# Attention and two MLPs on one core: fewer DMAs, a shorter warm-up, and VectorE casting the high part of v

## The chip, the cores and the metric

The kernel runs on one core of one Trainium2 chip. The metric is the device time of one execution in microseconds. Five engines work side by side, each through its own instructions in order: TensorE (matrix products, into PSUM), VectorE, ScalarE and GpSimd (element by element), and SyncE (SP), which here only issues DMAs.

## The reference

```
scores = q @ k^T / sqrt(64)                    # 2 x 12 heads, 448 x 448
scores = cap * tanh(scores / cap)
attn = softmax(scores) @ v                     # -> x, 896 tokens x 768
x = elu(x @ w_in1) @ w_out1                    # 768 -> 2048 -> 768
out = relu(x @ w_in2) ** 2 @ w_out2            # 768 -> 2048 -> 768
```

The weights are 64-bit floats; q, k, v are 32-bit.

## The kernel before

Every product is made of three: a value is split into a high part (cast to a shorter format, float32r) and a low part (value minus high part), and high x high, high x low and low x high are added in PSUM. ScalarE and VectorE make the parts.

The attention takes two heads at a time, a *pair*; there are 12, and two pairs share a *group* of loads. Round n of the loop at L572 holds, for pair n, tanh and exp on ScalarE (`tanh`, `exp`: e), the split of the probabilities on VectorE (`split_p`: cast ph, subtraction pl, in two parts) and the products with v on TensorE (`pv`, into po); for pair n + 1, the low part of k and q (`low`: kql), the two parts of v (`prep_v`: vh, vl) and the first scores (`scores`: sc); for pair n + 2, the transposition of k and q (`turn`, into the one PSUM tile pt, which `high` on ScalarE and `low` on VectorE read). The last block of v has 64 rows and goes its own way (`vs`, kz and qz are the like of k and q).

The softmax's denominators fall out of `pv` as an extra row. `pv_out(n - 1)` copies po to pvs on ScalarE and a DMA brings the row to 64 partitions (den). A round later `norm(n - 2)` takes the reciprocal on VectorE (rd), writes it to DRAM by a DMA (far) and reads it back to all partitions by two DMAs (bc). A round later still `norm_x(n - 3)` multiplies (xn) and splits x into xh and xl.

The order is written out by hand (`manual_schedule`): the text of the loop is the order on each engine. All DMAs but the very first are on SP's queue, in this order in a round: far and the two bc of `norm`, in rounds 2 to 6 one weight load (`ws.load`), den of `pv_out`, then the loads of `load_group`: k and q (with kz, qz) and the tail of v in even rounds, v in odd ones.

Weights come in chunks (`Stream`): a load, then six steps on VectorE and ScalarE that turn 64-bit floats into a high and a low part (and or absolute value, clamp, shift, sign, low, high, rest). Two chunks are worked whole on VectorE during the attention (`ws.whole`, the second in round 1, between `low` and the split of the probabilities), the others step by step (`ws.advance`). `prep_v` is on GpSimd: for n > 1 a copy of one column (gate) that waits for VectorE's pl, the cast vh and the subtraction vl. At the start `idle_products` are matrix products that nobody reads.

After round 11 the tail (L621 to L651) finishes pairs 9, 10 and 11 (`norm`, `norm_x`) among the first products of the first MLP (`mm_in`), which need x of all pairs at their end. From there on the MLPs run on TensorE with the weight chunks made beside them.

Of the kernel before, what the change touches and what calls it, by code (L numbers as in the profile page):

```python
# [26 lines left out]
def attention_moe_kernel(  # L27
# [63 lines left out]
    gate = one.tile([P, 1], F32, name="gate")  # L91
# [12 lines left out]
    def load_group(g, what="kqvw", pp=None, dma=nc.sync.dma_start):  # L104
# [6 lines left out]
        if g not in nat:  # L111
            nat[g] = {x: lp.tile([P, NFULL, 4, D], F32, name=x, tag=x) for x in "kq"}
            nat[g]["v"] = lp.tile([P, 4, NFULL, D], F32, name="v", tag="v")
# [19 lines left out]
        if "v" in what:  # L133
            for hh in range(h0, h0 + nh):
                dma(
                    nat[g]["v"][:, hh],
                    v[b, 2 * hp + hh, :NFULL * P].rearrange("(c p) d -> p c d", p=P),
                )
# [7 lines left out]
    def prep_v(n):  # L146
        if n >= len(pairs):
            return
        g, pp = divmod(n, 2)
        vh, vl = vhs[n % 3], vls[n % 3]  # L150
        if n > 1:


            nc.gpsimd.tensor_copy(gate, st["p", n - 2][1][:, NB - 2, S - 1:].bitcast(F32))
        vn = nat[g]["v"][:, 2 * pp:2 * pp + 2]
        h, l = (t.rearrange("p (c h) d -> p h c d", h=2)[:, :, :, :D] for t in (vh, vl))
        nc.gpsimd.tensor_copy(h, vn)
        nc.gpsimd.tensor_tensor(l, vn, h.bitcast(F32), op=ALU.subtract)
# [22 lines left out]

    def high(n):
        if n >= len(pairs):
            return
        st["qk", n] = [ap_.tile([P, 2, W], F32R, name=x, tag=x) for x in ("kqh", "kql")]
        nc.scalar.copy(st["qk", n][0], st["pt", n])

    def low(n):
        if n >= len(pairs):
            return  # L190
        h, l = st["qk", n]
        nc.vector.tensor_tensor(l, st["pt", n], h.bitcast(F32), op=ALU.subtract)
# [109 lines left out]
    def norm(n):  # L302


        if n < 0:
            return
        den = st["den", n]
        rd = ap_.tile([D, 2 * S // D], F32, name="rd", tag="rd")
        nc.vector.reciprocal(rd, den)
        far = dp.tile([D, 2 * S // D], F32, name="far", tag="far")  # L310
        nc.sync.dma_start(far, rd)
        bc = ap_.tile([D, 2, S], F32, name="bc", tag="bc")
        flat = far.rearrange("p s -> (p s)")
        for u in range(2):
            src = flat[u * S:(u + 1) * S].unsqueeze(0).to_broadcast([D, S])
            nc.sync.dma_start(bc[:, u], src)
        st["bc", n] = bc
# [25 lines left out]
    class Stream:  # L343
# [119 lines left out]
        def whole(self):  # L463

            self.alone = True
            self.open(self.done)
            emit(self.begin(self.done) + self.end(self.done))
            self.done += 1
            self.alone = False
            self.hold = 0  # L470
# [62 lines left out]
    with tc.manual_schedule():  # L533
# [24 lines left out]
        ws.whole()  # L558
# [13 lines left out]
        for n in range(np_):  # L572
# [11 lines left out]
            if n == 1:  # L584
                ws.whole()
# [3 lines left out]
            if n:  # L589
                turn(n + 2)  # L590
            else:
                idle_products(ps1.tile([P, 2, W], F32, name="po", tag="po"), 20)
            norm(n - 2)
            if 2 <= n < 7:
                ws.load()
# [3 lines left out]
            pv_out(n - 1)  # L599
            tanh(n, 3)  # L600
            exp(n, 1)
            emit(norm_x(n - 3))
            split_p(n, 0)
            scores(n + 1, 0)
# [9 lines left out]
            if n % 2:  # L614
                load_group((n + 3) // 2, "v")
            else:
                load_group(n // 2 + 2, "kq")
# [4 lines left out]
        late_kc = 2 * (KC - 1)  # L622
        emit(ws.advance())
# [4 lines left out]
        norm(np_ - 2)  # L628
# [3 lines left out]
        mm_in(0, 0, begun[0], xh, xl, kb[1:7:2])  # L632
        norm(np_ - 1)
        ws.settle()
        mm_in(0, 1, begun[1], xh, xl, kb[0::2])
        emit(norm_x(np_ - 2))
# [170 lines left out]
```

## Time and profile before

| | |
|---|---|
| time, median of 3 runs | 599.96 us (599.31 to 600.51) |
| the profiled execution | 600.64 us, its span 598.9 us |
| TensorE busy | 585.6 us (98% of the span) |
| VectorE busy | 425.2 us (71%) |
| ScalarE busy | 334.9 us (56%) |
| GpSimd busy | 38.9 us (6%) |
| SP's and ScalarE's DMAs | 64.76 MB, mean 108 GB/s |

The span runs from the first to the last instruction. Busy times are shares of the whole span; the attention (up to about 142 us) and the MLPs behind it have different loads. In the rows, PE is TensorE, DVE VectorE, ACT ScalarE, POOL GpSimd, SPq the queue of SP; a row of the timeline gives start, duration, engine, line, operation, destination and sources, shapes, and in brackets how long the engine had stood idle and what ended that.

### The profile page before, as it was taken

The page shows a single profiled execution, that of the slowest core. Times are in us where ns is not written, and L with a number is a line of the kernel's source. Part 1 is how long each engine was busy: PE and PEld are TensorE (multiplying, and loading weights), DVE is VectorE, ACT ScalarE, POOL GpSimd, SP SyncE. Part 2 cuts the span into 40 slices and gives each one's busy share as a digit, 9 for nine tenths or more (in the row PEclk, how much of TensorE's full clock was granted, in tenths as well). Part 3 has the DMA queues.
Part 4 walks back from the last instruction along what each step waited for, and adds up shares of the span by engine and source line. Part 5 has one row for each costly group of instructions (what it writes and reads, how often), then busy time and mean ns, then how long its engine had stood idle before and what let it go on. Part 6 is the DMA issues. An engine that isn't in the chain of part 4 may idle for free.

```text
span 598.9 us, 8667 instructions
## 1 busy us (share of the span) xinstructions
PE 585.6 (98%) x3084; PEld 530.2 (89%) x3084; DVE 425.2 (71%) x835; ACT 334.9 (56%) x484; POOL 38.9 (6%) x66
## 2 busy tenths in 40 slices
PE   8998989989999999999999999999999999999997
PEld 8876767678999999999999999999999999999997
DVE  4777799979999888675666567777767689991000
ACT  4899789934888777543333335666666645441000
POOL 3221212100000000000000000000000011230000
PEclk9999999999999999999999999999999999999999
DMA  5644642014444333243333434333344346622000
GB/s 132 157 117 115 154 115 73 22 60 132 124 134 137 120 108 89 66 129 116 111 101 111 125 105 133 105 106 109 111 125 118 106 112 187 185 84 105 24 24 34
DMA packets 82988, 64.76 MB, mean 108 GB/s; under 512 B 38656, under 2 KB 78848, under 8 KB 82944
## 3 DMA queue, kind: packets, MB, share of 16 engines
q1 hardware_dynamic: 81440, 63.58, 37.2%
q10 hardware_dynamic: 1504, 0.62, 0.4%
q8 instruction: 24, 0.39, 0.3%
q14 instruction: 20, 0.16, 0.1%
HBM read 61.34 MB, written 2.80 MB: 107 GB/s over the span
## 4 chain that ended last, share of the span: by engine, by line
PE 84%; DVE 5%; DMA 4%; SPq 3%; ACT 2%; issue 1%; ACTq 0%; DVEq 0%
PE acc L520 19%; PE acc L521 19%; PE acc L519 19%; PE acc L738 7%; PE acc L739 7%; PE acc L737 7%; PE po L287 5%; PE sc L235 3%; DMA den<-pvs 2%; DVE pl L264 1%; SPq L120 1%; DVE xn L329 1%; ACT e L244 1%; DVE ph L263 1%; PE pt L172 1%
## 5 line engine op out<-in xcount | busy, mean ns | idle before, releaser
L521 PE MATMUL acc<-xh,wl 128*128 128x448 f32 x384 | 139.6, 364 | 2.0 <-DVE wl L443 2.0
L520 PE MATMUL acc<-xl,wh 128*128 128x448 f32 x384 | 140.0, 364 | 0.2 <-DVE xl L336 0.2
L519 PE MATMUL acc<-xh,wh 128*128 128x448 f32 x384 | 139.7, 364 | 0.2 <-ACT xh L335 0.2
L448 ACT CAST wh<-wf 128x384 fp32r<-128x384 f32 (+2 forms) x114 | 57.9, 508 | 107.6 <-PE acc L520 83.7
L393 ACT ACTIVATE wf<-wst 128x384 f32<-128x384 f32 (+2 forms) x130 | 70.4, 542 | 62.5 <-DVE wl L443 35.7
L443 DVE TENSOR_TENSOR wl<-wf,wh 128x384 fp32r<-128x384 f32 (+2 forms) x116 | 63.9, 551 | 55.3 <-ACT wh L448 55.2
L521 PEld LDWEIGHTS acc<-xh,wl 128*128 128x128 f32 x384 | 72.1, 188 | 7.6 <-DVE wl L443 2.4
L519 PEld LDWEIGHTS acc<-xh,wh 128*128 128x128 f32 x384 | 72.1, 188 | 6.2 <-ACT xh L335 0.6
L520 PEld LDWEIGHTS acc<-xl,wh 128*128 128x128 f32 x384 | 72.1, 188 | 5.7 <-DVE xl L336 0.5
L434 DVE SCALAR_TENSOR_TENSOR wf<-wst,wf 128x384 uint32<-128x384 uint32 (+3 forms) x132 | 71.9, 545 | 0.1
L427 DVE SCALAR_TENSOR_TENSOR wf<-wst,wf 128x384 uint32<-128x384 uint32 (+3 forms) x132 | 71.5, 541 | 0.1
L520 PE MATMUL acc<-gl,wh 128*128 128x448 f32 x192 | 70.0, 365 | 0.0
L521 PE MATMUL acc<-gh,wl 128*128 128x448 f32 x192 | 70.0, 364 | 0.0
L519 PE MATMUL acc<-gh,wh 128*128 128x448 f32 x192 | 69.8, 364 | 0.0
L406 DVE TENSOR_SCALAR wf<-wf 128x384 uint32<-128x384 uint32 (+3 forms) x132 | 54.5, 413 | 0.7
L402 DVE TENSOR_SCALAR wf<-wf 128x384 f32<-128x384 f32 (+3 forms) x132 | 45.9, 347 | 7.3 <-ACT wf L393 7.3
L244 ACT ACTIVATE e<-sc,tsc 128x896 f32<-128x896 f32 (+1 forms) x48 | 43.4, 910 | 6.4 <-PE sc L235 6.4
L724 DVE COPY o<-acc 128x432 f32<-128x432 f32 (+1 forms) x8 | 4.5, 558 | 53.9 <-PE acc L739 49.2
L443 POOL TENSOR_TENSOR late<-wf,late 128x336 fp32r<-128x336 f32 x16 | 15.2, 953 | 414.1 <-ACT late L448 414.1
L738 PE MATMUL acc<-wl,gh 128*128 128x432 f32 x112 | 40.3, 359 | 0.0
L739 PE MATMUL acc<-wh,gl 128*128 128x432 f32 x112 | 40.1, 358 | 0.0
L737 PE MATMUL acc<-wh,gh 128*128 128x432 f32 x112 | 40.0, 357 | 0.0
(94 smaller groups left out, 966.0 us busy)
## 6 DMA issues: line engine op xcount, KB each, us to landing
wst<-in_moe_w_in_dram SPq DMA_DIRECT2D x63, 384.0 KB, 3.2
wst<-in_moe_w_out_dram SPq DMA_DIRECT2D x24, 384.0 KB, 3.2
wst<-in_moe_w_out_dram SPq DMA_DIRECT2D x16, 432.0 KB, 3.3
wst<-in_moe_w_out_dram SPq DMA_DIRECT2D x16, 336.0 KB, 2.9
wst<-in_moe_w_out_dram SPq DMA_DIRECT2D x12, 256.0 KB, 2.7
bc<-far SPq DMA_DIRECT2D x24, 112.0 KB, 2.8
v<-in_v_dram SPq DMA_DIRECT2D x24, 96.0 KB, 2.7
k<-in_k_dram SPq DMA_DIRECT2D x15, 128.0 KB, 3.0
```

Of the source, the lines that this page charges most:

```text
L393: nc.scalar.activation(self.f[i], hi.bitcast(F32), AF.Abs)
L406: v.tensor_scalar(fb, fb, 3, 0x3FFFFFFF, op0=ALU.logical_shift_left, op1=ALU.bitwise_and)
L427: v.scalar_tensor_tensor(out=fb, in0=hi, scalar=0xC0000000, in1=fb, op0=ALU.bitwise_and, op1=ALU.bitwise_or,)
L434: v.scalar_tensor_tensor(out=fb, in0=lo, scalar=29, in1=fb, op0=ALU.logical_shift_right, op1=ALU.bitwise_or,)
L443: (v if dst is None else nc.gpsimd).tensor_tensor(wl, self.f[i], wh.bitcast(F32), op=ALU.subtract)
L448: (v.tensor_copy if self.alone else nc.scalar.copy)(wh, self.f[i])
L519: nc.tensor.matmul(acc, w[0], x[0], start=first, stop=False)
L520: nc.tensor.matmul(acc, w[0], x[1], start=False, stop=False)
L521: nc.tensor.matmul(acc, w[1], x[0], start=False, stop=last)
L737: nc.tensor.matmul(acc, gh[:, f, gs], w[0], start=a, stop=False)
L738: nc.tensor.matmul(acc, gh[:, f, gs], w[1], start=False, stop=False)
L739: nc.tensor.matmul(acc, gl[:, f, gs], w[0], start=False, stop=z)
```

## The change

- `prep_v`: for n > 1 the cast vh is made by VectorE, right behind the second part of `split_p`; the gate is gone; GpSimd makes vl.
- v is laid out by block and head instead of head and block, and a group's v comes in three DMAs (one a block) instead of four (one a head). The first group is loaded in halves and so takes six instead of four.
- From round 2 on, q of a group is loaded with v in the odd round, k alone in the even one.
- `norm` reads the reciprocals back with one DMA instead of two.
- `high` and `low` work on 960 columns instead of 1024.
- 9 idle products instead of 20 in round 0.
- The second whole weight chunk is cut in two: three instructions at the end of round 1, the other four in round 2 behind `low`.
- The weight load of rounds 2 to 6 is issued behind den instead of ahead of it.
- In the tail, `norm` of pair 10 comes first, and the product xn of pair 10 and the rest of a weight chunk come ahead of `norm` of pair 11.

```diff
-            nat[g] = {x: lp.tile([P, NFULL, 4, D], F32, name=x, tag=x) for x in "kq"}
-            nat[g]["v"] = lp.tile([P, 4, NFULL, D], F32, name="v", tag="v")
+            nat[g] = {x: lp.tile([P, NFULL, 4, D], F32, name=x, tag=x) for x in "kqv"}
...
-            for hh in range(h0, h0 + nh):
+            for c in range(NFULL):
                 dma(
-                    nat[g]["v"][:, hh],
-                    v[b, 2 * hp + hh, :NFULL * P].rearrange("(c p) d -> p c d", p=P),
+                    nat[g]["v"][:, c, h0:h0 + nh],
+                    v[b, hs, c * P:(c + 1) * P].rearrange("h p d -> p h d"),
                 )
...
-        if n > 1:
-            nc.gpsimd.tensor_copy(gate, st["p", n - 2][1][:, NB - 2, S - 1:].bitcast(F32))
-        vn = nat[g]["v"][:, 2 * pp:2 * pp + 2]
-        h, l = (t.rearrange("p (c h) d -> p h c d", h=2)[:, :, :, :D] for t in (vh, vl))
-        nc.gpsimd.tensor_copy(h, vn)
+        vn = nat[g]["v"][:, :, 2 * pp:2 * pp + 2]
+        h, l = (t.rearrange("p (c h) d -> p c h d", h=2)[:, :, :, :D] for t in (vh, vl))
+        (nc.vector if n > 1 else nc.gpsimd).tensor_copy(h, vn)
         nc.gpsimd.tensor_tensor(l, vn, h.bitcast(F32), op=ALU.subtract)
...
+    def used(t):
+        return t.rearrange("p u w -> p (u w)")[:, :W + S]
...
-        nc.scalar.copy(st["qk", n][0], st["pt", n])
+        nc.scalar.copy(used(st["qk", n][0]), used(st["pt", n]))
...
-        h, l = st["qk", n]
-        nc.vector.tensor_tensor(l, st["pt", n], h.bitcast(F32), op=ALU.subtract)
+        h, l, t = (used(x) for x in (*st["qk", n], st["pt", n]))
+        nc.vector.tensor_tensor(l, t, h.bitcast(F32), op=ALU.subtract)
...
-        flat = far.rearrange("p s -> (p s)")
-        for u in range(2):
-            src = flat[u * S:(u + 1) * S].unsqueeze(0).to_broadcast([D, S])
-            nc.sync.dma_start(bc[:, u], src)
+        flat = far.rearrange("p s -> (p s)").unsqueeze(0)
+        nc.sync.dma_start(bc.rearrange("p h s -> p (h s)"), flat.to_broadcast([D, 2 * S]))
...
-            if n == 1:
-                ws.whole()
+            if n == 2:
+                emit(second[3:])
...
-                idle_products(ps1.tile([P, 2, W], F32, name="po", tag="po"), 20)
+                idle_products(ps1.tile([P, 2, W], F32, name="po", tag="po"), 9)
             norm(n - 2)
-            if 2 <= n < 7:
-                ws.load()
...
             pv_out(n - 1)
+            if 2 <= n < 7:
+                ws.load()
...
             split_p(n, 0)
+            if n == 1:
+                second = ws.whole()
+                emit(second[:3])
...
-                load_group((n + 3) // 2, "v")
+                load_group((n + 3) // 2, "qv" if n > 1 else "v")
             else:
-                load_group(n // 2 + 2, "kq")
+                load_group(n // 2 + 2, "k" if n else "kq")
                 load_group(n // 2 + 1, "w" if n else "")
...
+        norm(np_ - 2)
         emit(ws.advance())
         ws.held = True
         split_p(np_ - 1, 1)
         mm_in(0, 0, begun[0], xh, xl, kb[6::2])
         pv(np_ - 1, 1)
-        norm(np_ - 2)
         pv_out(np_ - 1)
         emit(norm_x(np_ - 3))
         emit(ws.advance())
         mm_in(0, 0, begun[0], xh, xl, kb[1:7:2])
+        x, x_high, x_low = norm_x(np_ - 2)
+        x()
+        ws.settle()
         norm(np_ - 1)
-        ws.settle()
         mm_in(0, 1, begun[1], xh, xl, kb[0::2])
-        emit(norm_x(np_ - 2))
+        x_high()
+        x_low()
```

## Rows read from the trace of the kernel before

**Rows 1.** The page: the chain that ended last, by engine

```profile
PE 84%; DVE 5%; DMA 4%; SPq 3%; ACT 2%; issue 1%; ACTq 0%; DVEq 0%
```

**Rows 2.** Busy times by stretch: length, engines, granted clock, DMA share, GB/s

```profile
34.82:45.50 10.68, 10.68 (x68) 8.54 (x68) 8.32 (x10) 10.06 (x11) 1.67 (x3) 1.00 0.52 126
...
56.48:65.73 9.25, 8.02 (x35) 6.13 (x36) 8.14 (x11) 5.61 (x6) 1.64 (x3) 0.82 0.54 136
...
103.49:112.32 8.83, 8.72 (x49) 6.03 (x49) 8.56 (x11) 8.26 (x8) 1.65 (x3) 1.00 0.10 30
...
120.79:142.25 21.46, 18.86 (x88) 15.08 (x86) 17.37 (x34) 6.92 (x11) 0.00 (x0) 1.00 0.27 83
```

**Rows 3.** TensorE's timeline: the first scores of pairs 3 and 4

```profile
36.55 0.47 PE L235 MATMUL sc<-kqh 64*128 64x448 f32 x2
...
45.04 0.47 PE L235 MATMUL sc<-kqh 64*128 64x448 f32 x2
```

**Rows 4.** Waits from 35 to 120 us (total, times, longest), and VectorE's timeline

```profile
DVE rd L309 <- DMA den<-pvs: 8.7, 5, 2.6
...
43.13 0.23 DVE L309 RECIPROCAL rd<-den 64x14 f32<-64x14 f32 x1 [2.02 <-DMA den<-pvs]
...
54.11 0.23 DVE L309 RECIPROCAL rd<-den 64x14 f32<-64x14 f32 x1 [2.56 <-DMA den<-pvs]
```

**Rows 5.** Timeline of VectorE, rounds 8 to 10, and one row of GpSimd's

```profile
92.44 1.21 DVE L329 TENSOR_TENSOR xn<-pvs,bc 64x448 f32<-64x448 f32 x2
...
103.49 1.09 DVE L263 CAST ph<-e 128x1792 fp32r<-128x1792 f32 x1
...
108.32 1.22 DVE L192 TENSOR_TENSOR kql<-pt,kqh 128x1024 fp32r<-128x1024 f32 x1
...
109.60 1.72 DVE L329 TENSOR_TENSOR xn<-pvs,bc 64x448 f32<-64x448 f32 x2
...
109.17 1.01 POOL L158 TENSOR_TENSOR vl<-v,vh 128x384 fp32r<-128x384 f32 x1
```

**Rows 6.** Timeline of SP's queue from den of pair 1 to den of pair 2

```profile
39.29 0.50 SPq L299 DMA_DIRECT2D den<-pvs  x1
...
45.85 1.29 SPq L141 DMA_DIRECT2D vs<-in_v_dram  x2
47.23 0.56 SPq L311 DMA_DIRECT2D far<-rd  x1
48.99 1.11 SPq L316 DMA_DIRECT2D bc<-far  x2
...
50.84 0.50 SPq L299 DMA_DIRECT2D den<-pvs  x1
```

**Rows 7.** VectorE's timeline: two instructions on 384 columns, with one and two operands

```profile
26.89 0.36 DVE L448 CAST wh<-wf 128x384 fp32r<-128x384 f32 x1
...
144.45 0.55 DVE L443 TENSOR_TENSOR wl<-wf,wh 128x384 fp32r<-128x384 f32 x1
```

**Rows 8.** The start: timelines of TensorE, SP's queue and GpSimd

```profile
13.26 4.62 PE L196 MATMUL po<-ident 128*128 128x128 f32 x40
...
20.51 2.08 SPq L135 DMA_DIRECT2D v<-in_v_dram  x4
...
24.64 0.51 POOL L157 CAST vh<-v 128x384 fp32r<-128x384 f32 x1 [2.23 <-DMA v<-in_v_dram]
```

**Rows 9.** The tail: timelines of ScalarE, SP's queue, VectorE and TensorE

```profile
129.35 0.91 ACT L296 COPY pvs<-po 128x896 f32<-128x896 f32 x1 [3.20 <-PE po L287]
...
129.94 1.09 SPq L316 DMA_DIRECT2D bc<-far  x2
131.41 0.51 SPq L299 DMA_DIRECT2D den<-pvs  x1
...
134.65 0.23 DVE L309 RECIPROCAL rd<-den 64x14 f32<-64x14 f32 x1 [3.07 <-DMA den<-pvs]
...
135.34 0.47 PE L521 MATMUL acc<-xh,wl 128*128 128x448 f32 x1 [1.98 <-DVE wl L443]
```

More of the change, by code (lines that the diff above doesn't have):

```diff
@@ L90, in attention_moe_kernel @@
     vls = [one.tile([P, NB - 1, P], F32R, name=f"vl{i}") for i in range(3)]
-    gate = one.tile([P, 1], F32, name="gate")
     vss = [one.tile([P, 2, P], F32, name=f"vs{i}") for i in range(2)]
@@ L463, in whole, with alone @@
         def whole(self):
-            self.alone = True
-            self.open(self.done)
-            emit(self.begin(self.done) + self.end(self.done))
+            i = self.done
             self.done += 1
-            self.alone = False
-            self.hold = 0
+            def alone(step):
+                self.alone = True
+                step()
+                self.alone, self.hold = False, 0
+            steps = [lambda: self.open(i)] + self.begin(i) + self.end(i)
+            return [lambda step=step: alone(step) for step in steps]
         def start(self):
@@ L556, in attention_moe_kernel @@
         turn(1)
-        ws.whole()
+        emit(ws.whole())
         accs = itertools.count()
@@ L583, in attention_moe_kernel @@
             low(n + 1)
-            if n == 1:
-                ws.whole()
+            if n == 2:
+                emit(second[3:])
             scores(n, 2)
```

## The prediction

> **What bounds the kernel now.** I first read the chain that ended last, by engine: TensorE holds 84% of it [rows 1]. A busy TensorE says little by stage, so I cut the span at the start of each round's big cast on VectorE (ph of 128x1792, L263) and read the busy times in those stretches [rows 2]. From the handover at 142.25 us on, TensorE runs without a gap worth naming and the change touches nothing there; so whatever is won is the time by which the handover comes earlier, one to one.
>
> In the attention rounds before it the order is another. Laid end to end on TensorE, one round is 8.49 us: the scores of one pair start at 36.55, those of the next at 45.04, with no gap between [rows 3]. The rounds from 34.82 to 112.32 us are eight and take 77.5 us, 9.69 each: 10.68, 10.98, 9.25, 10.93, 8.83, 9.16, 8.84, 8.83, of which the first, the third and the last stand in [rows 2]. Two things on VectorE make them longer. In five of the eight VectorE stands before the reciprocal rd and waits for the denominators that a DMA brings, 8.7 us in all [rows 4]. In the three others it never waits and the round is 8.83. There the two products xn take 1.72 us; in a round where GpSimd's subtraction vl is over before them they take 1.21 [rows 5]. The subtraction at 109.17 lies on top of xn at 109.60. So a VectorE round without wait or collision is 8.83 - 0.51 = 8.32 us.
>
> Why den is late is read on SP's queue [rows 4, 6]. The reciprocal ran at 43.13, yet its DMA far was issued at 47.23: SP was busy with the k, q and w loads of the round, up to vs at 45.85. Then far lands, two bc go out, then a weight load, and only then den at 50.84, for which VectorE waited 2.56 us at 54.11. From den to den that round cost SP 11.5 us (39.29 to 50.84), with 11 loads in it.
>
> **The change, part by part.** *SP's queue.* Loads per round: before 11 and 4 in turn, after 7 and 7 (k with w, q with v; v in three DMAs for four). One bc for two, and the weight load behind den. At about 0.6 us an issue [rows 6] a round of SP is 7 x 0.6 = 4.2, far to bc 1.76 (47.23 to 48.99), bc 0.6, den 0.6, weight load 0.65: 7.8 us, under a VectorE round. den then goes out some 2.6 us after rd and lands some 3 us later, 3 us before the next rd. I take all 8.7 us of waiting as gone. Next late after it is VectorE's own order.
>
> *The v cast.* Ten casts of 128x384 come onto VectorE, each between split_p and kql. The trace has none with these operands. A cast of 384 elements in one run takes 0.36, a two-operand instruction of 384 takes 0.55 [rows 7]; with some 0.04 to the next start, 0.40 to 0.59. All fast casts of the trace read and write one run per partition; this one reads three runs and writes six. So I take 0.59 and keep 0.40 for the range. The Trainium skill bears on this, "VectorE: DVE Perf Modes", section "What auto-detection actually checks": the two-element mode of a single-source instruction wants the outermost counts of source and destination both even or equal. With 3 runs against 6 it would refuse the mode; if both sides keep their three blocks it would grant it, and the sum would be that of the first rival. No row of before shows such a cast.
>
> *GpSimd.* The gate and its cast go; the subtraction starts when VectorE's cast ends, lies beside kql (1.22, L192) and is over before xn. kql reads PSUM, and its 1.22 is the same in every round although GpSimd always works beside it [rows 5], so I price no collision: the 0.51 of xn goes. If the subtraction ended late, xn would give up to 0.51 back per round.
>
> *960 columns for 1024* in kql: 64 of 1024 columns less, at most 0.076 of its 1.22; I take 0.07. On ScalarE 0.05, worth nothing since ScalarE waits for pvs's product in each round. A VectorE round after: 8.32 + 0.59 - 0.07 = 8.84; with the cheap cast 8.65. TensorE's 8.49 stays below both.
>
> *The start.* Nine idle products for 20: the 20 took 4.62 us [rows 8], eleven are 2.5. Scores of pair 1 come earlier, but turn(2) behind them waits for q of group 1, and two more v DMAs of group 0 stand ahead of it in SP's queue (0.55 of them before q). So this gains nothing; TensorE waits some 2 us there instead. What it costs if the clock falls: in the stretch from 56.48 the granted clock was 0.82 after TensorE had stood still [rows 2]; ScalarE and VectorE have more than that lost time (some 1 us) to spare here.
>
> The v cast of pair 2 now stands in VectorE's order ahead of kql(2), and behind it ph(1,0), turn(3) on TensorE (kql frees pt) and scores(2). It waits for v of group 1. Before, four DMAs from 20.51 and GpSimd released at 24.64 [rows 8], 2.6 after the last issue at 22.07. After: 1.1 later for the two DMAs more, 0.5 earlier for three instead of four: 25.2. From there VectorE does the two casts (2 x 0.59), kql twice (2 x 1.07), the four steps of split_p (4.83, from 103.49 to 108.32 [rows 5]), the three first instructions of the weight chunk (1.2), its other four (2.05, by [rows 7], no longer beside GpSimd) and rd (0.2): 11.6, so ph(2,0) starts at 36.8. Before it was 34.82 (the start of the first stretch of [rows 2]). The start costs 2.0 us; the bound is 1.5 (cheap cast) to 3.
>
> *Eight rounds*: 8 x 8.84 = 70.7 for 77.5, and the last round before the tail unchanged. ph(11,0) comes 77.5 - 70.7 - 2.0 = 4.8 us earlier.
>
> *The tail.* pvs(11) is done at 130.26, but den(11) goes out at 131.41, since bc(10) fills SP from 129.94 [rows 9]. With the reciprocal of pair 10 moved ahead of the weight steps (0.2 more ahead of split_p(11,1), which has over 1 us to spare), far(10) and bc(10) are through by about 127.5 and den(11) leaves about 1.0 earlier. TensorE's 1.98 us of idling at 135.34 goes as well: wl stood behind rd(11), which waited 3.07 for den(11), and x of pair 10 and wl now come ahead of rd(11). That gap alone is worth nothing, for the last x sets the end; it only lets TensorE be done in time. The one bc carries twice the bytes: both xn wait for all of it. Between no more than now (gain 1.5, as xn no longer waits twice) and a landing 1 us longer (0.5), I take 1.0 as sum.
>
> **Sum**: 4.8 + 1.0 = 5.8 us. The profiled execution has 598.9 us of span and 1.74 around it, 600.64, which is 0.7 above the median of 599.96; the saving is a difference inside that execution, and I take it off the median: 594.2 us.
>
> **Rivals.** *The cheap cast.* At 0.40 eight rounds save 8 x 0.19 and the start 0.4: 1.9 us more, 592.3. For it: every fast cast that is there runs at this rate. Against: the broken runs.
>
> *den stays half late.* The waits move from SP's issues to the DMAs themselves: far or den land behind the q and v loads, which are now in the same round. For it: of the waits, 0.75 fell in a round with only four loads ahead. Half of 8.7 stays: 594.2 + 4.35 = 598.5.
>
> *q comes too late, the other side.* q of groups 3, 4 and 5 is asked for at the end of the odd round and turned in the next; before it had two rounds. By the budget above it is issued by about rd + 6.1 and there at rd + 9 if it lands in 3 us; turn starts (0.97 before 45.04, with rd at 43.13) at the earliest 0.9 after the next rd, rd + 9.8. From 3.8 us of landing on TensorE stands before turn, with scores and tanh of the next pair behind it, three times. At 6.3 us that is 3 x 2.5 = 7.5: 601.7, slower. Against: the v load of [rows 8] landed in 2.6.
>
> *The DMAs do not shrink the queue* (an issue of one bc takes as long as two did): 0.5 us of SP per round, and the budget of 7.8 still fits; this changes nothing.
>
> **How the numbers follow.** Forecast 45%, cheap cast 22%, den half late 20%, q late 6%, the rest is mixtures. The forecast with its bounds runs from 593 to 596; to leave out no more than 2 in 10 the range takes in the cheap cast and the half-late den: 591.6 to 598.6. A measurement of this kernel can tell some 0.2%, 1.2 us, from no change: below 598.8 is faster. Forecast, cheap cast and two thirds of the half-late case: 0.84 with mixtures; within 0.2%: 0.09; slower 0.07.
>
> **What would show it.** Casts vh on VectorE of 0.55 (or 0.36); the rd rows without waits; xn pairs of 1.2 everywhere; ph starts 8.8 apart from ph(2,0) near 36.8 on; den on SP within 3 us of far; the handover to the dense part near 136.5; no 2 us gap of TensorE in the tail, and a new one near 18 us. Waits of vh on the v DMA after the start, of turn on q, or of rd on den would prove me wrong, and so would rounds near TensorE's 8.5.

## The result, and the profile after

The changed kernel takes 595.07 us (median of 4 runs, 594.1 to 595.82) where the kernel before took 600.1 beside it (599.31 to 600.51): a ratio of 0.991, with a 95% interval of 0.9889 to 0.9931. The profiled execution of after is the fastest of its four: 594.1 us, with a span of 592.3 us.

First the page's chain of work that ended last, by engine, to be laid beside [rows 1]:

```profile
PE 90%; DMA 3%; DVE 3%; SPq 2%; ACT 1%; issue 1%; POOL 0%; ACTq 0%; POOLq 0%; DVEq 0%
```

TensorE's share is up from 84 to 90 in a hundred; what the chain lost is time on VectorE and behind DMAs. Where it was lost shows in the busy times by stretch, again cut at the starts of the big cast ph (length, engines, granted clock, DMA share, GB/s):

```profile
45.76:54.42 8.66, 8.66 (x52) 6.48 (x50) 8.44 (x13) 8.19 (x9) 1.01 (x1) 1.00 0.60 152
106.39:114.99 8.60, 8.17 (x44) 6.01 (x43) 7.68 (x12) 8.16 (x10) 0.00 (x0) 1.00 0.13 48
114.99:135.28 20.29, 18.70 (x86) 15.01 (x85) 17.25 (x34) 6.76 (x11) 0.00 (x0) 1.00 0.28 86
```

Of the eight rounds from ph of pair 2 on the first is 8.60 us and each of the others 8.66 or 8.67, where those of the kernel before went from 8.83 to 10.98; the second row is the last round. VectorE (the third busy time) works 8.44 of 8.66. One of these rounds on VectorE's timeline, with rd of the round before it, which answers to [rows 4, 5]:

```profile
43.42 0.22 DVE L309 RECIPROCAL rd<-den 64x14 f32<-64x14 f32 x1
...
50.55 0.55 DVE L153 CAST vh<-v 128x384 fp32r<-128x384 f32 x1
51.01 1.15 DVE L192 TENSOR_TENSOR kql<-pt,kqh 128x960 fp32r<-128x960 f32 x1
52.08 0.22 DVE L309 RECIPROCAL rd<-den 64x14 f32<-64x14 f32 x1
52.23 1.19 DVE L327 TENSOR_TENSOR xn<-pvs,bc 64x448 f32<-64x448 f32 x2
```

No row has a wait in brackets: rd finds its denominators there, and the pair xn takes 1.18 or 1.19 in each of the eight rounds. The new cast lasts 0.55, but the next instruction starts 0.46 after it. On SP's queue the round reads so (beside [rows 6]):

```profile
46.11 0.50 SPq L311 DMA_DIRECT2D far<-rd  x1
47.95 0.47 SPq L314 DMA_DIRECT2D bc<-far  x1
48.51 0.54 SPq L299 DMA_DIRECT2D den<-pvs  x1
49.11 0.58 SPq L372 DMA_DIRECT2D wst<-in_moe_w_in_dram  x1
49.74 1.58 SPq L118 DMA_DIRECT2D q<-in_q_dram  x3
51.36 0.64 SPq L122 DMA_DIRECT2D qz<-in_q_dram  x1
52.05 1.70 SPq L133 DMA_DIRECT2D v<-in_v_dram  x3
53.85 0.49 SPq L311 DMA_DIRECT2D far<-rd  x1
```

den goes out 2.4 us behind far, and the seven loads of the round (wst not counted) are through before the next far, 7.7 us after the first. But far itself stands behind loads: rd ran at 43.42 and its far left at 46.11, the next rd at 52.08 and its far at 53.85. So den leaves 5.1 us behind its round's rd and 3.6 us before the rd that needs it. These DMAs of den land 2.9 us after their issue (median in this trace from 35 to 120 us), so that by estimate 0.7 us are to spare.

The start, beside [rows 8], on SP's queue and on VectorE:

```profile
21.18 1.58 SPq L133 DMA_DIRECT2D v<-in_v_dram  x3
...
26.01 0.55 DVE L153 CAST vh<-v 128x384 fp32r<-128x384 f32 x1 [7.04 <-DMA v<-in_v_dram]
...
27.54 1.08 DVE L263 CAST ph<-e 128x1792 fp32r<-128x1792 f32 x1
...
37.16 1.02 DVE L263 CAST ph<-e 128x1792 fp32r<-128x1792 f32 x1
```

VectorE stands 7.04 us for v of group 1, and ph of pair 2 starts 2.3 later than before. And the tail, beside [rows 9] (ScalarE, SP's queue, VectorE, TensorE):

```profile
123.57 0.91 ACT L296 COPY pvs<-po 128x896 f32<-128x896 f32 x1 [3.14 <-PE po L287]
124.50 0.49 SPq L299 DMA_DIRECT2D den<-pvs  x1
127.41 0.22 DVE L309 RECIPROCAL rd<-den 64x14 f32<-64x14 f32 x1
...
132.72 1.25 DVE L327 TENSOR_TENSOR xn<-pvs,bc 64x448 f32<-64x448 f32 x2 [2.58 <-DMA bc<-far]
134.62 0.47 PE L521 MATMUL acc<-xh,wh 128*128 128x448 f32 x1 [1.15 <-ACT xh L333]
135.28 0.47 PE L522 MATMUL acc<-xl,wh 128*128 128x448 f32 x1 [0.19 <-DVE xl L334]
```

rd of pair 11 no longer waits, TensorE's gap of 1.98 us behind wl is gone (it stands 1.15 for xh of pair 11 instead), and the handover comes at 135.28 for 142.25, 6.97 us earlier. The two profiled executions differ by 6.54 (600.64 and 594.1): 0.43 us more lie behind the handover. The medians differ by 5.0, since after's four times are 594.1, 594.34, 595.79 and 595.82, and the profile shows one of the lower pair.

### The profile page after: what moved, and what is told of

It is laid out like the page before. It is cut to its first block, busy times and chain, and to the rows that moved or that the text cites. A ratio compares the mean times of both kernels' runs of the same rounds, so it can differ in the third digit from the quotient of the medians.

```text
span 592.3 us, 8596 instructions
## 1 busy us (share of the span) xinstructions
PE 583.4 (98%) x3062; PEld 528.0 (89%) x3062; DVE 425.0 (72%) x845; ACT 334.2 (56%) x484; POOL 32.1 (5%) x46
## 3 DMA queue, kind: packets, MB, share of 16 engines
q1 hardware_dynamic: 80432, 63.58, 36.8%
## 4 chain that ended last, share of the span: by engine, by line
PE 90%; DMA 3%; DVE 3%; SPq 2%; ACT 1%; issue 1%; POOL 0%; ACTq 0%; POOLq 0%; DVEq 0%
PE acc L522 19%; PE acc L523 19%; PE acc L521 19%; PE po L287 8%; PE acc L746 7%; PE acc L745 7%; PE acc L747 7%; PE sc L235 4%; PE pt L168 1%; DMA q<-in_q_dram 1%; SPq L118 1%; DVE xn L327 1%; DMA far<-rd 1%; DMA bc<-far 1%; DMA qz<-in_q_dram 0%
## 5 line engine op out<-in xcount | busy, mean ns | idle before, releaser
L252 ACT ACTIVATE e<-e,capt 128x1792 f32<-128x1792 f32 (+1 forms) x24 | 38.6, 1609 | 0.8
```

## The experiments

All variants compute the whole reference. They were run in four groups, each with the kernel before beside it (600.83, 600.31, 600.27 and 600.33). A column below is a stretch of the profiled execution, cut at ph of pairs 2 and 10 and at the handover to the dense part; the last but one is the profiled execution's time less its handover.

| kernel | ph of pair 2 | eight rounds | last round and tail | handover | time behind it | median us, ratio to before (95%) |
|---|---|---|---|---|---|---|
| before | 34.82 | 77.50 | 29.93 | 142.25 | 458.39 | 599.96 |
| b_again | 34.47 | 76.61 | 30.45 | 141.53 | 458.27 | 599.94, 0.999 (0.9977 to 1.0003) |
| after | 37.16 | 69.23 | 28.89 | 135.28 | 458.82 | 595.07, 0.991 (0.9889 to 0.9931) |
| b_queue | 36.04 | 71.12 | 28.55 | 135.71 | 458.59 | 593.85, 0.9889 (0.9876 to 0.9903) |
| b_cast | 35.72 | 76.61 | 28.28 | 140.61 | 458.39 | 599.0, 0.9972 (0.9962 to 0.9982) |
| a_castback | 38.02 | 70.89 | 29.02 | 137.93 | 458.82 | 597.05, 0.9939 (0.992 to 0.9959) |
| a_qk | 37.32 | 72.06 | 28.99 | 138.37 | 458.87 | 597.25, 0.9949 (0.9933 to 0.9965) |
| a_tail | 38.18 | 69.25 | 28.96 | 136.39 | 458.81 | 594.73, 0.9905 (0.9889 to 0.992) |
| a_20 | 37.35 | 69.24 | 29.25 | 135.84 | 458.80 | 594.39, 0.9904 (0.9886 to 0.9922) |
| a_n2gps | 38.07 | 69.39 | 29.29 | 136.75 | 458.81 | 595.0, 0.9907 (0.9892 to 0.9923) |
| a_n2gps_20 | 36.25 | 69.24 | 29.22 | 134.71 | 458.81 | 593.38, 0.9895 (0.9871 to 0.992) |
| a_headmajor | 37.46 | 68.51 | 30.29 | 136.26 | 458.81 | 594.14, 0.9897 (0.9883 to 0.9911) |
| a_hm_late | 36.71 | 67.87 | 29.24 | 133.82 | 458.85 | 594.19, 0.9898 (0.9879 to 0.9916) |
| a_best2 | 36.33 | 68.11 | 29.37 | 133.81 | 458.84 | 592.07, 0.9867 (0.9847 to 0.9887) |

The handover is the first product that needs the low part of x of pair 11. The time behind it is the same within 0.6 us in all of them: the handover decides, one to one. So where two medians lie too near each other, the stretches still tell what moved. They also show a limit: after, a_qk and a_tail have the same text up to pair 3, and their ph of pair 2 starts at 37.16, 37.32 and 38.18. A start is repeated to within 1 us only.

### b_queue: the DMAs alone, on the kernel before

v by block, one bc, q with v from round 2 on, the weight load behind den; the casts, the idle products, the weight chunk and the tail stay as they were.

```diff
-            nc.sync.dma_start(bc[:, u], src)
+        nc.sync.dma_start(bc.rearrange("p h s -> p (h s)"), flat.to_broadcast([D, 2 * S]))
...
-                load_group((n + 3) // 2, "v")
+                load_group((n + 3) // 2, "qv" if n > 1 else "v")
```

> The kernel before with the DMA part of the change alone (q with v in the odd rounds, v by block in three DMAs, one bc, the weight load behind den); gate, GpSimd's cast, the warm-up, the whole weight chunk and the tail stay as before. Theory (the queue of SP makes den late): the waits of rd for den, 8.7 us in five rounds, go; every round then has GpSimd's subtraction on top of xn and is 8.83 us, eight rounds 70.6 instead of 77.5: 6.9 us less, 593.1 us, about as much as the whole change. Rival (the gain is the cast that moved to VectorE and the collision it removes): at most 1 us less, 599.

Measured: 593.85 us, not to be told from after. VectorE's waits from 35 to 120 us, one pair xn, and den of pair 11 on SP's queue:

```profile
DVE rd L308 <- DMA den<-pvs: 0.9, 2, 0.8
...
51.12 1.70 DVE L326 TENSOR_TENSOR xn<-pvs,bc 64x448 f32<-64x448 f32 x2
...
125.16 0.49 SPq L298 DMA_DIRECT2D den<-pvs  x1
```

Of 8.7 us of waiting 0.9 are left, and the collision of xn with GpSimd stays (1.70 for 1.19). The eight rounds lose 6.4 of their 77.5 us by this alone. Last round and tail, in their old order, lose 1.4 of 29.93 (den of pair 11, the last row, comes back below), and the start is 1.2 later. At the handover this makes 6.54 us, of the 6.97 of the whole change. The SP queue is the cause, and nearly the whole gain. All other parts together take 1.9 us more out of the rounds and give back 1.1 at the start and 0.3 in last round and tail; the times show no gain of theirs.

### b_cast: VectorE's cast alone, on the kernel before

The gate goes and vh is cast by VectorE for n > 1, with v still laid out by head.

```diff
-            nc.gpsimd.tensor_copy(gate, st["p", n - 2][1][:, NB - 2, S - 1:].bitcast(F32))
...
-        nc.gpsimd.tensor_copy(h, vn)
+        (nc.vector if n > 1 else nc.gpsimd).tensor_copy(h, vn)
```

> The kernel before with the v cast on VectorE alone (n > 1, no gate), DMAs and the layout of v (head by block) as before. Theory: the waits for den stay, only the three rounds without a wait get shorter (by the collision of 0.51 less the cast), and at the start VectorE stands before the cast of pair 2 until v lands at 24.6 us with kql and the whole weight chunk behind it, about 1.5 us: 600 to 602 us. Rival (the cast is the gain): 596 or less. The cast's price: source and destination have even outermost counts here (2 heads), so 0.36 us if the broken runs of the changed kernel were what cost 0.55; 0.55 if every cast with gaps in its destination costs that.

Measured: 599.0, 1.8 us under before beside it, between the two; neither number holds. The gain is small against the noise: before run once more, below, comes out at 0.999 (0.9977 to 1.0003), and the two intervals overlap a little. VectorE's waits from 35 to 120 us, the cast, and in the tail den and rd of pair 11:

```profile
DVE rd L304 <- DMA den<-pvs: 7.5, 4, 3.1
...
40.67 0.35 DVE L152 CAST vh<-v 128x384 fp32r<-128x384 f32 x1
...
130.87 0.51 SPq L294 DMA_DIRECT2D den<-pvs  x1
133.22 0.23 DVE L304 RECIPROCAL rd<-den 64x14 f32<-64x14 f32 x1 [1.39 <-DMA den<-pvs]
```

The waits for den stay, and no gain of the cast is shown in the eight rounds (76.61 for 77.50, but before run once more has 76.61 too). It takes 0.35 to 0.36 in this layout. The start is 0.9 later, and the gain lies in the tail, whose text is that of before: last round and tail are 28.28 for 29.93. den of pair 11 was at rd 2.35 us after its issue, where it was 3.24 in [rows 9].

### b_again: before once more

> The kernel before once more, unchanged, for a second profile of its tail. In the first profile last round and tail took 29.93 us (ph of pair 10 to the handover): far of pair 10 was 2.50 us before its bc, den of pair 11 was at rd 3.24 us after its issue, and rd waited 3.07. With the same tail text the kernel with VectorE's cast alone took 28.28 (1.72, 2.35 and 1.39). Theory A (those landings are late in some executions only, and the tail's saving in the changed kernel is no effect of the change): 28.3 to 29.2 here, far to bc near 1.7, rd's wait 1 to 2 us, and the handover between 140.6 and 141.6 with eight rounds near 77.5. Theory B (the old tail is slow with this kernel's timing each time): 29.6 to 30.2, far to bc 2.4 or more, rd's wait near 3, handover near 142.3; then a part of 1.0 us of the tail's saving is the change's, by what shifts these DMAs.

Measured: 599.94. SP's queue, VectorE and TensorE in the tail, and below them two of the microseconds behind TensorE's wait (length, engines, granted clock, DMA share, GB/s):

```profile
126.21 0.47 SPq L311 DMA_DIRECT2D far<-rd  x1
128.73 1.09 SPq L316 DMA_DIRECT2D bc<-far  x2
130.20 0.51 SPq L299 DMA_DIRECT2D den<-pvs  x1
133.31 0.23 DVE L309 RECIPROCAL rd<-den 64x14 f32<-64x14 f32 x1 [2.97 <-DMA den<-pvs]
134.01 0.47 PE L521 MATMUL acc<-xh,wl 128*128 128x448 f32 x1 [1.84 <-DVE wl L443]
```

```profile
135.53:137.53 2.00, 2.00 (x7) 1.78 (x6) 1.93 (x6) 0.00 (x0) 0.00 (x0) 0.50 0.32 85
```

far to bc 2.52 and rd's wait 2.97 are as Theory B has them: the old tail's landings are late with this kernel's timing, not in one execution only. Last round and tail, 30.45, lie above even B's range, and for another reason. Behind the wait of 1.84 for wl the granted clock fell to 0.50, which is the lower of its two levels (1.2 GHz), and TensorE's products came 0.37 us apart instead of 0.20 for some 3 us. So TensorE reached x of pair 11 without a pause, but late: the handover is 1.31 us behind the start of xl of pair 11, where it was 0.68 in before (141.57 to 142.25). The clock cost 0.6 us here, by this estimate. In before the same wait, 1.98, was followed by a clock of 1.00; what made the difference no run shows.

### a_castback: the cast back on GpSimd, in the changed kernel

```diff
+            nc.gpsimd.tensor_copy(gate, st["p", n - 2][1][:, NB - 2, S - 1:].bitcast(F32))
...
-        (nc.vector if n > 1 else nc.gpsimd).tensor_copy(h, vn)
+        nc.gpsimd.tensor_copy(h, vn)
```

> The changed kernel with the high part of v cast by GpSimd again in all rounds, behind its one-column gate; the DMAs, the 960 columns, 9 idle products, the cut weight chunk and the tail stay as changed. Theory (VectorE's cast costs 0.47 a round and saves the collision of 0.51 with xn; in the start it also puts VectorE behind v's landing at 26.0): rounds of 8.7 to 8.8 with xn of 1.7, start 0.5 to 1.5 us earlier (ph of pair 2 at 35.7 to 36.7), so the time within 0.8 us of the changed kernel, rather below (594.3 to 595.1). Rival (as the prediction has it, the cast on VectorE is nearly free by the round and the start is set by ScalarE and TensorE): start the same, 37.1, and rounds 8.83: time 1.2 to 1.5 above the changed kernel.

Measured: 597.05, 2.0 above after, though the two intervals overlap a little; the eight rounds take 70.89 for 69.23. On VectorE:

```profile
27.60 1.09 DVE L266 CAST ph<-e 128x1792 fp32r<-128x1792 f32 x1 [4.37 <-PE po L290]
...
52.86 1.76 DVE L330 TENSOR_TENSOR xn<-pvs,bc 64x448 f32<-64x448 f32 x2
```

xn takes 1.76 again in the rounds without a wait, and three short waits for den come back (1.3 us in all). The start isn't earlier, though VectorE no longer waits for v: it now waits for TensorE. So the rival holds in the rounds: with the queue mended, VectorE sets the round, and the cast there is worth 1.7 us of rounds. The start, 38.02 for the rival's 37.1, is within what a start varies.

### a_qk: q again with k

```diff
-                load_group((n + 3) // 2, "qv" if n > 1 else "v")
+                load_group((n + 3) // 2, "v")
...
-                load_group(n // 2 + 2, "k" if n else "kq")
+                load_group(n // 2 + 2, "kq")
```

> The changed kernel with q of groups 3 to 5 loaded together with k in the even rounds, as before; v by three DMAs, one bc and the weight load behind den stay. SP's loads per round are then 11 and 3 in turn for 7 and 7. Theory (den is late because SP issues too many loads in one round): the four more issues of the even rounds take 4 x 0.6 = 2.4 us; far, bc and den of every second round go out 2.4 us later, minus the slack of den (it lands some 3 us before rd); so den waits of 0 to 1 us in three or four of the rounds from 46 to 115, and the time 0.5 to 2 us above the changed kernel (595.6 to 597). Rival (the one bc, the weight load and the v DMAs do it, the split of q is not needed): no waits, rounds stay 8.66, time within 0.3.

Measured: 597.25, 2.2 above after, a little more than the theory's upper end. VectorE's reciprocals:

```profile
54.08 0.23 DVE L309 RECIPROCAL rd<-den 64x14 f32<-64x14 f32 x1 [1.75 <-DMA den<-pvs]
...
72.37 0.23 DVE L309 RECIPROCAL rd<-den 64x14 f32<-64x14 f32 x1 [0.88 <-DMA den<-pvs]
```

Two waits, not the three or four shorter ones of the theory, in rounds behind one with eleven loads; these rounds are 10.52 and 9.63 for 8.66. So, with the rest in place, the four issues moved into the other round are about a third of what the DMAs bring (2.2 of the 7.0 by which b_queue is faster than before beside it). The rest is with v, bc and the order of the weight load, which were not separated.

### a_tail: the tail in its old order

```diff
-        norm(np_ - 2)
         emit(ws.advance())
         ws.held = True
...
+        norm(np_ - 2)
         pv_out(np_ - 1)
...
-        x()
-        ws.settle()
         norm(np_ - 1)
+        ws.settle()
```

> The changed kernel with the tail's old order: norm of pair 10 behind split_p and pv of pair 11, and the product xn of pair 10 and the rest of the weight chunk behind norm of pair 11. Theory (the tail's gain of 1.0 to 1.2 us comes from den of pair 11, which no longer stands behind bc of pair 10): den of pair 11 leaves SP 1.0 to 1.5 us later against pvs of pair 11, rd of pair 11 waits 2.5 to 3 us for it, TensorE stands some 2 us behind wl, ph of pair 11 to the handover takes 21.4 for 20.3, and the time is 1.0 to 1.3 above the changed kernel. Rival (with one bc for two the queue is free soon enough in either order): 20.3 to 20.8, time 0 to 0.5 above.

Measured: 594.73; last round and tail 28.96 for 28.89. SP's queue and VectorE:

```profile
124.92 0.45 SPq L314 DMA_DIRECT2D bc<-far  x1
125.56 0.48 SPq L299 DMA_DIRECT2D den<-pvs  x1
...
128.30 0.23 DVE L309 RECIPROCAL rd<-den 64x14 f32<-64x14 f32 x1 [1.50 <-DMA den<-pvs]
```

den of pair 11 leaves 0.94 after the start of its pvs, as in after (0.93): bc of pair 10, one DMA now, is issued at 124.92, takes SP 0.45 for the 1.09 of two, and is through at 125.37, before pvs is (125.53). rd waits 1.50, and it costs nothing that reaches the end. The new order gains nothing that can be shown, once the rest of the change is there.

### a_20 and a_n2gps: 20 idle products, or the cast of pair 2 on GpSimd

```diff
-                idle_products(ps1.tile([P, 2, W], F32, name="po", tag="po"), 9)
+                idle_products(ps1.tile([P, 2, W], F32, name="po", tag="po"), 20)
```

> The changed kernel with 20 idle products at the start as before, for 9; nothing else is undone. In the trace of the changed kernel TensorE waits near 18 us for q three times (0.37, 0.72, 0.22) and the products behind that take 1.73 and 1.70 us at 19.99 and 21.52 where those of before took 1.06 and 0.99. Theory (what the fewer products cost is the clock): with 20 the waits are filled, the products behind take about 1.0 each, scores, products with v and tanh of the first rounds come about 1 us earlier; VectorE's own order, which waits for v at 26.0, takes part of that up; ph of pair 2 starts 0.5 to 1 us earlier than 37.16, and the time is 0.5 to 1 us below the changed kernel (594.1 to 594.6 for 595.07). Rival (v's landing sets the start whatever TensorE does, as the prediction said): ph of pair 2 at 37.2, time within 0.3 of the changed kernel. Second rival (the 2.5 us more of idle products delay turn of pair 2, for which q would be there by 20 us): up to 1 us slower, 596.

```diff
-        (nc.vector if n > 1 else nc.gpsimd).tensor_copy(h, vn)
+        (nc.vector if n > 2 else nc.gpsimd).tensor_copy(h, vn)
```

> The changed kernel with the v cast of pair 2 alone left on GpSimd (VectorE casts from pair 3 on). Theory (VectorE's 7.0 us before that cast at the start is what the start costs): ph(1,0) starts near 24.5 instead of 27.5 and ph(2,0) near 35 instead of 37.2; 1.5 to 2.5 us less than the changed kernel, 593. Rival (ScalarE and TensorE hold the start anyway, by q and the first scores): within 0.5 us of the changed kernel, 595.

Measured: 594.39 and 595.0; neither can be told from after, and ph of pair 2 is at 37.35 and 38.07 for 37.16. The stretch from 20 to 24 us in after, and its first products with v:

```profile
20.00:24.00 4.00, 4.00 (x13) 3.43 (x12) 0.00 (x0) 3.66 (x3) 1.51 (x2) 0.57 0.60 161
...
19.99 1.73 PE L287 MATMUL po<-ph,vh 128*128 128x448 f32 x4
```

the same stretch in a_20, with VectorE's cast behind it:

```profile
20.00:24.00 4.00, 3.95 (x23) 3.16 (x23) 0.00 (x0) 3.58 (x4) 1.52 (x2) 1.00 0.57 152
...
20.17 1.04 PE L287 MATMUL po<-ph,vh 128*128 128x448 f32 x4
...
26.20 0.55 DVE L153 CAST vh<-v 128x384 fp32r<-128x384 f32 x1 [7.58 <-DMA v<-in_v_dram]
```

and ph of pair 1 in a_n2gps:

```profile
28.04 1.49 DVE L263 CAST ph<-e 128x1792 fp32r<-128x1792 f32 x1 [4.87 <-PE po L287]
```

After three waits for q the granted clock of after is 0.57 in this stretch, so mostly at the lower of the two levels (1.2 GHz), and four products take 1.73; with 20 idle products it is 1.00 (2.4 GHz) and they take 1.04. This helps nothing as long as VectorE stands for v until 26.2. And when VectorE doesn't stand for v, as in a_n2gps, it stands for those slow products (granted clock 0.50 from 20 to 24 us there).

### a_n2gps_20: both

> The changed kernel with two parts of the start undone together: the cast vh of pair 2 on GpSimd, and 20 idle products for 9. Either one alone moved the time by less than 0.7 us. In the run with GpSimd's cast alone VectorE stood 4.87 us before ph of pair 1 for TensorE's products po, which came late and slow (1.83, 1.70 and 1.58 us); in the run with 20 idle products alone those products took 1.04, 0.97 and 0.98, but VectorE stood 7.58 us for v. Theory (two things, each of them enough, hold the start: v's landing on VectorE, TensorE's late and slow products): together they go; po of pair 0 is done near 25.7, ph of pair 1 starts near 26.2 and ph of pair 2 near 36.0, as in the kernel before with the DMA part alone (36.04); 1.2 us earlier than 37.16 in the changed kernel, so 593.5 to 594.2. Rival (the start is held by something third, such as v's landing through TensorE's products with v of pair 1): ph of pair 2 at 37 or later, 595.

Measured: 593.38 (five of six runs from 593.06 to 593.52, with granted clocks of 0.999 and 1.000; the sixth 597.81, with 0.994); on VectorE:

```profile
25.68 1.09 DVE L263 CAST ph<-e 128x1792 fp32r<-128x1792 f32 x1 [3.00 <-PE po L287]
...
36.25 1.02 DVE L263 CAST ph<-e 128x1792 fp32r<-128x1792 f32 x1
```

ph of pair 1 starts 1.9 earlier than in after, ph of pair 2 0.9. The second is no more than a start varies, but a_best2, below, has the same start and repeats both (25.95 and 36.33), and every variant of after with only one of the two undone, or none, is later (27.29 or more and 36.71 or more). So the theory holds in the traces: two things held the start, each of them enough. Against after the times alone don't settle it, as their intervals overlap.

### a_headmajor and a_hm_late: v by head and block

The DMAs stay three, by block; only the tile in SBUF is laid out by head, so that the cast reads one run per partition.

```diff
-            nat[g] = {x: lp.tile([P, NFULL, 4, D], F32, name=x, tag=x) for x in "kqv"}
+            nat[g] = {x: lp.tile([P, NFULL, 4, D], F32, name=x, tag=x) for x in "kq"}
+            nat[g]["v"] = lp.tile([P, 4, NFULL, D], F32, name="v", tag="v")
```

> The changed kernel with v kept head by block in SBUF (same three DMAs a group), so that the cast reads one run of 384 and writes 2 x 3 blocks. Theory (unequal, odd outermost counts cost the cast its fast rate): the cast takes 0.36 instead of 0.55, a round 8.49 to 8.5 (TensorE's own) instead of 8.66: 1.3 to 1.9 us less, 593.3. Rival (any gap in the destination costs it): 0.55 as now, 595.

Measured: 594.14. The group of the cast from 35 to 120 us (busy, mean ns of one, idle before) in after and, below it, in a_headmajor; then VectorE in a_headmajor's last round:

```profile
L153 DVE CAST vh<-v 128x384 fp32r<-128x384 f32 x8 | 4.4, 545 | 0.0
```

```profile
L154 DVE CAST vh<-v 128x384 fp32r<-128x384 f32 x8 | 2.8, 353 | 0.0
...
113.10 0.36 DVE L401 TENSOR_SCALAR wf<-wf 128x384 f32<-128x384 f32 x1 [2.11 <-ACT wf L392]
```

The cast falls from 545 to 353 ns, and six of the eight rounds to between 8.40 and 8.48. The two others are 8.74 and 9.01, as rd waits for den again (0.6 us in all). And the last round is 10.05: the tail's first weight steps stand on ScalarE behind exp, and on VectorE ahead of xn and ph, which wait with them. In a_hm_late these steps were moved behind the split of the last round:

```diff
-            if last:
-                emit(ws.start())
             tanh(n, 2)
...
             split_p(n, 0)
+            if last:
+                emit(ws.start())
```

> The changed kernel with v laid out by head and block (the cast takes 0.36 for 0.55) and, in the last round alone, the first steps of the streamed weights (two absolute values on ScalarE, clamp and shift on VectorE) moved from ahead of the third tanh to behind the split of the probabilities. With the layout alone rounds were 8.47 but the last one 10.05, with VectorE standing 2.11 us for ScalarE's absolute value behind exp, and the whole gained about 1 us only. Theory (the saved 0.19 a round is lost in the last round to that wait): last round 8.5 to 8.9, handover 1.2 us earlier than the 136.26 with the layout alone, time 0.8 to 1.3 below it, 592.9 to 593.3. Rival (ScalarE, whose round is itself near 8.5, is the bound at the end, and the moved steps only come later in the tail): handover within 0.4, time 593.8 to 594.3.

Measured: last round and tail 29.24 for 30.29, as the theory has it. Yet that is no better than after's 28.89: the last round falls to 7.71, and the moved steps come later, as the rival says, in a tail of 21.53 for after's 20.29. The time shows no gain: the six runs go from 592.67 to 596.06, and their median is that of the layout alone. The profiled one is the fastest, and the only one with a granted clock of 1.000; the others have 0.994 to 0.997.

### a_best2: layout, start and last round together

> All three together on the changed kernel: v laid out by head and block, the cast of pair 2 on GpSimd with 20 idle products, and the last round's first weight steps behind the split. Theory (they act in three different stretches, so their gains add): start 1.2, eight rounds 8 x 0.19 = 1.5, last round not lost: ph of pair 2 near 36.0, rounds of 8.47, handover near 132.7, and 592.0 to 592.7. Rival (ScalarE and TensorE, which need 8.5 a round, already set the rounds at 8.47, and what the start gains is taken back by waits for q or den in the first rounds): 593.3 to 594.1.

Measured: 592.07 us, 0.9867 (0.9847 to 0.9887) of before: the best median of all here, 1.3% under before. Its interval lies below that of after, if only just, and overlaps that of b_queue. One round of the profiled execution:

```profile
79.03:87.50 8.47, 8.47 (x52) 6.55 (x51) 8.25 (x12) 8.13 (x9) 1.02 (x1) 1.00 0.53 124
```

Seven rounds from 8.41 to 8.48, start 36.33, handover 133.81: 1.5 us under after, where the theory's 132.7 had 2.6. The start gained 0.8 for 1.2, the rounds 1.1 for 1.5, and last round and tail took 0.5 more than in after. What the rounds lost there is one wait for den of 0.31 at 68.22, in the one round of 8.87.

## Why the prediction was right, and where its terms were off

The forecast was 594.2, in a range of 591.6 to 598.6; the median is 595.07 and the profiled execution 594.1. The main mechanism, SP's queue, was right and is shown; that the number lies within 1 us is in part luck, as the terms below show.

*What bounds the kernel* held: the time behind the handover is the same within 0.6 us in every run, and VectorE with its waits for den set the rounds.

*SP's queue.* All waits for den were to go, and all went. The budget of 7.8 us of SP a round is 7.7 in the rows of SP above. Its margin was wrong: den was to go out 2.6 us behind rd and land 3 us before the next one, but it goes out 5.1 us behind, since far stands behind the loads of the round before, and by the estimate above has 0.7 to spare. Where the round gets shorter, waits of 0.3 and 0.6 us come back (a_best2, a_headmajor). b_queue shows that the queue alone does it, a_qk that the split of q is needed for a part of it.

*The v cast.* Its duration, 0.55, was right, and b_cast and a_headmajor, which read one run and also write six, take 0.35 to 0.36. That a source in pieces is slow as such doesn't hold, though: the first step of a weight chunk reads every second 32-bit word and is as fast.

```profile
30.67 0.35 DVE L387 TENSOR_SCALAR wf<-wst 128x384 uint32<-128x384 uint32 x1
```

The Trainium skill's rule on the outermost counts ("VectorE: DVE Perf Modes", section "What auto-detection actually checks") agrees with all these rows; no run tried three blocks on both sides, where by that rule the cast would be fast. The failing step is the 0.04 added to the next start: the next instruction starts 0.46 behind the cast, not 0.59. This makes 0.13 of the 0.18 by which the round is shorter than the 8.84 of the sum; the eight rounds saved 8.3 us, not 6.8.

*The collision* went, as priced: xn 1.19 in each round, and 1.76 in a_castback. *960 columns* gave 0.06 for 0.07 (from kql to xn 1.28 in [rows 5], 1.22 now).

*The start* was to cost 2.0, with ph of pair 2 at 36.8; it came at 37.16, and 2.3 dearer. v was at VectorE at 26.0, not 25.2, and from there on it took 11.15 for 11.6: the last of its three issues began near 22.2 (21.18 and two thirds of 1.58), and v was there 3.8 later, not 2.6. The wait of TensorE near 18 us came, and the lower clock after it; "ScalarE and VectorE have more than that to spare" was right only because VectorE stood for v anyway, as a_n2gps shows. Beside a_n2gps_20, which has neither (36.25), VectorE's cast alone (a_20) makes the start 1.1 us later, the fewer idle products alone (a_n2gps) 1.8, and both (after) 0.9: each by itself costs what both cost, within the 1 us that a start varies. The other 1.2 of the 2.3 b_queue has too, by the DMAs alone. The cut weight chunk was not tried alone.

*The tail* is where the number agrees and a step of the mechanism failed, so that the agreement is luck. ph of pair 11 to the handover took 1.2 less where 1.0 was forecast. What had to go was read rightly: den of pair 11 stood behind bc of pair 10. Counted from ph of pair 11, den leaves SP at 10.62 us in before, 10.64 in b_again and 9.51 in after. But the sum put this down to the new order, and den leaves as early with the old one, at 9.53 in a_tail and 9.52 in b_queue; the stretch to the handover is as short there too (20.36 and 20.07 beside 20.29 in after and 21.46 in before). So the DMA part brings the gain, and of the order none is shown. By the rows of a_tail it is the one bc for two (two, at 1.09, would hold SP 0.5 us past the end of pvs there); it was not run alone. It isn't the only way: b_cast, with the old order and two bc, is the fastest (den at 9.83, handover at 19.57). There the small DMAs land earlier: far to bc of pair 10 took 1.72, where it took 2.50 and 2.52 in the two profiles of before. Why they land late in before, with far 1.80 behind a weight load there as in b_cast, is open. "That gap alone is worth nothing", of TensorE behind wl, held in before, where TensorE still stood 0.24 for xh of pair 11; in b_again the clock fell behind the gap, and it cost 0.6.

So the sum of 5.8 was met by errors that partly cancel: 1.5 better in the rounds, 0.3 worse at the start, 0.1 worse in the last round and 0.2 better in the tail make the 6.97 of the handover, and 0.43 are lost behind it, in no step of the sum. These 0.43 are in all variants of after, a_tail and a_castback too, and in half in b_queue. They have no one place: laid product by product beside before, TensorE in after is 0.19 later 85 us behind the handover, 0.47 at 327 us and 0.31 at its last product, and never waits in between; why is open. The profiled execution saves 0.7 more than forecast and the median 0.9 less, as half of after's runs are 1.5 us above the others. The start differs by as much as 1.0 us between executions of the same text, which would fit, but no run ties the two together.

*The rivals.* The cheap cast didn't come, and where it was brought about (a_headmajor) it gave less than 1.9 us: the rounds won 0.7 for 1.5, because of two waits for den, and the last round, behind ScalarE, took 1.4 back. den half late: no wait was left. q too late: TensorE waited for q 0.7 us in all behind 35 us, far from the 2.5 a time of the rival.

## What to carry to other kernels

When several engines hand short results on through one DMA queue, lay out one round of that queue, issue by issue, and see that each round stays under the round of the engine that bounds, and how much is left between a result's landing and its use. How evenly loads are spread over the rounds counts beside their number (a_qk: 2.2 us at the same number). That a step's saving comes out at its size doesn't show its mechanism; undoing that one step does. Two causes that each hold the same stretch show no gain when taken away one by one, so take them away together before either is called free.

## What of the hardware had not been expected

- On VectorE the next instruction starts before the profile lets the one before end: a cast of 545 ns had its successor 0.46 us after its start (50.55 and 51.01), and kql of 1.15 us had rd 1.07 later. For these two a price by durations is too high by 0.08 to 0.09. An instruction that reads the one before it starts behind its end instead: xh 0.03 behind xn, pl 0.10 behind ph (53.45 and 46.94, after).
- The same 384 elements, cast from one run per partition or from three, take 353 and 545 ns; three DMAs can write either layout. One of the weight steps reads every second word of its source and takes 352.
- Small DMAs land late in a way that repeats and that no row explains: den of pair 11 was at rd 3.24 and 3.11 us after its issue in two executions of before, 2.35 in b_cast, with the DMAs of the tail in the same order ahead of it.
- A wait of TensorE of nearly the same length was followed by the lower clock once and not the other time: 1.84 us and then 0.50 for two microseconds and more in b_again, 1.98 us and then 1.00 in before, with the same instructions.
